# Attention and a two-layer MLP on one core: six instead of eight column groups of the first layer beside attention

## The chip, the core and the metric

The kernel runs on one core of a Trainium2 chip. TensorE (PE) multiplies, VectorE (DVE), ScalarE (ACT) and GpSimd (POOL) do the element-wise work, and SyncE (SP) issues nearly all DMAs. The metric is the time of one execution in microseconds (us); the median of several runs counts.

## What is computed

```python
scores = scale * q @ k.T            # 4 batches, 8 heads, 576 tokens, head size 64
scores = where(block_i >= block_j, scores, -1e9)      # causal in blocks of 64 tokens
attn = exp(scores - max) / (sum + 1e-9)
x = (attn @ v), heads side by side  # 2304 tokens x 512
h = x @ w_in;  x = (max(h, 0) + alpha * min(h, 0)) @ w_out     # 512 -> 2048 -> 512
h = x @ w2_in; out = (h * sigmoid(1.702 * h)) @ w2_out         # 512 -> 2048 -> 512
```

The weights arrive as 64-bit floats and are narrowed on the chip. Every product of the two layers is made from split numbers: a high part that the PE takes exactly and a low part, so that three products (high by high, high by low, low by high) stand for one.

## The kernel before

**Attention** runs in 20 passes of two heads. The first eight (batch 0, in two halves) turn their exponentials with the PE: `score` writes PSUM tile `sc`, `soft` takes the minimum (DVE) and the exponential (ACT), `turn_e` transposes the exponentials into PSUM, `turn_out` copies them out (ACT), `pv_t` multiplies by `v`. The other twelve passes turn them by a DMA transpose (`pt<-hl`, three a pass, 36 in all) and `pv` reads them. At the start the PE has little to do and 104 dummy products (`warm`) are put in.

**The first layer** has 16 column groups of 128. The first `NA` of them, eight, are computed beside attention, for eight blocks of 288 tokens, whenever the attention has finished a block: `gemm1` (tile `h`, 12 matmuls a group) and `g2_half` (tile `x`). These matmuls of 288 columns are what fills the PE between the steps of attention; the text calls them the fill. Their partial result goes to DRAM (`xa`). The other eight groups come after attention, two groups (a pair) at a time, for units of 512 tokens (four whole ones and a half): `first_half` and `second_half` form seven products of 256 columns in place of eight (tiles `ga`, `ep`), `snap` and `sums` put them together, and `g2` multiplies on into four PSUM banks `acc`. At a unit's end `block_out` loads the partial result (`o<-xa`), adds it to the four banks on DVE and stores the sum (`x2s<-o`). There are two `o` buffers for the four banks, so the loads for the third and fourth bank wait until the first two stores have landed.

**The second layer** works like the second part of the first, with all 16 groups as eight pairs.

The combined weights of the seven products are made by `comb`, stored to DRAM (`wc<-wc`) and loaded again (`ws<-wc`, 256 KB each). Before, the four pairs of the first layer are loaded once and stay in place; those of the second layer are loaded again for each unit.

`narrow` turns a 64-bit weight tile into 32 bits: one ACT operation and three on DVE. `gate` computes the activation: for the second layer a sigmoid on ACT and a product on DVE.

**The order** on each engine is fixed when the kernel is built. `at` notes every step with a due time plus a number from the table `SHIFT`; `arrange` is a list scheduler that goes through a model of the five engines and always takes the ready step with the smallest number. SP's DMAs too stand in one such order, and a DMA that waits for its data holds up those behind it.

Of the kernel before, what the change touches and what calls it, by code (L numbers as in the profile page):

```python
# [52 lines left out]

ORDER = {
# [6 lines left out]
    "comb 2": 232.8, "comb 3": -27.9, "first": 27.3, "gate": -98.0, "gate 0": -19.6, "gate 2": 67.8,  # L61
    "gemm1": 68.3, "gemm1 0": 171.6, "gemm2": 27.6, "half": 66.8, "half 0": 164.8, "half out": -68.7,
    "half out 0": 90.2, "high": 37.1, "load alpha": -25.6, "load k": 97.5, "load k 0": -174.1, "load q": 31.3,
    "load q 0": 127.5, "load v": -31.6, "load v 0": 140.7, "load w": -98.2, "load w 2": -24.0,
    "load w 3": 13.9, "load wc": -36.6, "load x": 132.4, "narrow": 100.5, "narrow 2": 19.6, "narrow 3": 96.5,
    "norm": 32.7, "norm 0": 111.8, "out": 26.7, "out t": -34.5, "prep out": 33.8, "prep out 0": 43.8,
    "prep t": 63.8, "prep t 0": -50.0, "prep v": 92.2, "pv": -64.1, "pv out": -63.9, "pv t": 43.2,
    "rest": -30.8, "scale t": 6.7, "score": -10.7, "score 0": -166.4, "second": 27.7, "setup": -15.8,
    "setup 2": -29.8, "snap": 1.4, "soft": -70.8, "soft 0": 17.8, "split g": -167.4, "split g 0": 68.9,
    "split g 2": 45.0, "split w": -71.7, "split w 2": 46.4, "split w 3": 58.0, "split x": 35.9,  # L70
    "split x 2": 84.1, "sum out": -41.5, "sum t": 28.5, "sums": -46.2, "turn": -70.2, "turn out": -30.2,
    "warm": 50.2,
# [5 lines left out]
def kernel(  # L78
# [19 lines left out]
    NA = 8  # L98
# [133 lines left out]
    def gate(key, layer, f):  # L232
        ps, n = pend[key, f]
        g = gbuf(key, "g")[:, 0:n]
        to = ps if key[0] else g
        if layer == 0:
            act.activation(out=g, in_=ps, func=ACTF.Relu, scale=-1.0)
            dve.scalar_tensor_tensor(out=to, in0=g, scalar=nalph[:, f:f + 1], in1=ps, op0=ALU.mult, op1=ALU.add)  # L238
        else:
            act.activation(out=g, in_=ps, func=ACTF.Sigmoid, scale=1.702)  # L240
            dve.tensor_tensor(out=to, in0=g, in1=ps, op=ALU.mult)
        pend[key, f] = (to, n)
# [10 lines left out]
    def plan_g1(n, key, layer, f, lo):  # L253
        z = " 0" if key[1] < 2 else ""
# [24 lines left out]
    def plan_block(i, where):  # L279
# [4 lines left out]
        for z, (d, e) in enumerate(G2):  # L284
            x = " 0" if i < 2 else ""
# [207 lines left out]
    def turn_out(i, g, t):  # L493
        ps, n = st.pop(("et", i, g, t)), len(TURN[g][t])
        if n == 8:
            st[i, "pt", g, t] = two.tile([128, 9, 128], F32, tag="pt", bufs=PTB, name="pe")
            hi_part(st[i, "pt", g, t][:, 0:8], ps)
# [112 lines left out]
    for u, (i, g, prods, part) in enumerate(slots):  # L610
        n = place_[u]
        lag = 5 if i >= N0 else 4
        x = " 0" if i < NTP else ""
# [638 lines left out]
```

## Time and profile before

| | us |
|---|---|
| median of 3 runs | 1004.37 (1003.66 to 1005.82) |
| the profiled execution | 1003.02 |
| its span, first to last instruction | 1001.2 |
| PE busy | 978.1 (98%) |
| DVE, ACT, POOL busy | 651.0, 533.7, 351.9 |

The span falls into five stretches. To 117.4 us the first eight passes run; to 350.5 us the passes with DMA transposes; to 413.9 us only what is left of the fill; to 621 us the pairs of the first layer; and then the second layer. "Busy" of the PE overlaps from one matmul to the next, so the pace of a run of matmuls is read from their starts.

### The profile page before, as it was taken

What the parts mean: (1) busy time and instruction counts of PE and PEld (TensorE: products, weight loads), DVE (VectorE), ACT (ScalarE), POOL (GpSimd) and SP (SyncE); (2) the same over time, 40 slices, a digit from 0 to 9 for tenths busy, and PEclk for the clock granted to TensorE, in tenths of its full rate; (3) what the DMA queues carried; (4) which work ended last, traced back from release to release, by engine and by line L of the source; (5) the groups of instructions that cost most, each with busy time, mean ns of one, the idle gap of its engine ahead of it and who ended that gap; (6) DMA issues with size and microseconds to landing.
All of it is one profiled execution on the core that took longest, in us unless ns stands there. A gap on an engine that the chain in (4) does not pass through costs nothing.

```text
span 1001.2 us, 21866 instructions
## 1 busy us (share of the span) xinstructions
PE 978.1 (98%) x8260; PEld 859.7 (86%) x8260; DVE 651.0 (65%) x1301; ACT 533.7 (53%) x1284; POOL 351.9 (35%) x396
## 2 busy tenths in 40 slices
PE   8999999999999999999999999999999999999998
PEld 5777787787788999999899889889999899899997
DVE  4788877786577566778778797887535534534332
ACT  4778777775777455565445555555423423433232
POOL 4346243442625156753426535233311311211000
PEclk9999999999999999999999999999999999999999
DMA  9635999999986866654656688987745756564360
GB/s 191 161 124 142 209 211 205 206 204 213 192 201 131 169 210 218 243 190 167 206 171 230 231 274 273 315 302 248 238 160 181 256 165 198 195 207 145 98 208 32
DMA packets 234648, 198.31 MB, mean 198 GB/s; under 512 B 146224, under 2 KB 172848, under 8 KB 234544
## 3 DMA queue, kind: packets, MB, share of 16 engines
q1 hardware_dynamic: 233216, 196.60, 69.2%
q8 instruction: 65, 1.06, 0.5%
q10 hardware_dynamic: 1328, 0.33, 0.2%
q14 instruction: 39, 0.32, 0.1%
HBM read 136.32 MB, written 40.89 MB: 177 GB/s over the span
## 4 chain that ended last, share of the span: by engine, by line
PE 81%; DMA 9%; ACT 3%; DVE 2%; POOL 2%; SPq 1%; issue 1%; POOLq 0%; ACTq 0%; DVEq 0%
PE acc L918 28%; PE ga L843 15%; PE ep L843 11%; PE h L223 7%; PE pv L599 3%; PE sc L448 3%; DMA pt<-hl 3%; PE x L268 3%; PE x L269 3%; PE x L270 3%; DMA wc<-wc 3%; PE pv L524 2%; PE tp L388 1%; DMA o<-xa 1%; PE s L448 1%
## 5 line engine op out<-in xcount | busy, mean ns | idle before, releaser
L918 PE MATMUL acc<-wh,gs 128*128 128x512 f32 x576 | 184.5, 391 | 2.1 <-DVE o L928 2.1
L843 PE MATMUL ga<-xc,ws 128*128 128x256 f32 x1368 | 184.2, 283 | 0.0
L843 PEld LDWEIGHTS ga<-xc,ws 128*128 128x128 f32 x1368 | 176.5, 191 | 4.6
L843 PE MATMUL ep<-xc,ws 128*128 128x256 f32 x936 | 130.7, 283 | 0.0
L918 PEld LDWEIGHTS acc<-wh,gs 128*128 128x128 f32 x576 | 108.3, 188 | 24.6 <-DVE o L928 2.9
L869 POOL TENSOR_TENSOR v<-u,v 128x256 f32<-128x256 f32 x48 | 40.5, 843 | 239.4 <-ACT v L868 239.3
L843 PEld LDWEIGHTS ep<-xc,ws 128*128 128x128 f32 x936 | 120.4, 192 | 0.4
L918 PE MATMUL acc<-wl,gs 128*128 128x512 f32 x288 | 112.6, 391 | 0.0
L867 ACT ACTIVATE u<-ga 128x512 f32<-128x512 f32 x48 | 28.6, 596 | 146.3 <-PE ga L843 146.3
L918 PE MATMUL acc<-gs,wh 128*128 128x512 f32 (+1 forms) x320 | 92.2, 371 | 2.1 <-DVE o L928 2.1
L891 DVE TENSOR_TENSOR u<-ep,v 128x256 f32<-128x256 f32 x48 | 20.2, 421 | 112.0 <-PE ep L843 111.7
L143 POOL TENSOR_TENSOR gs<-g,gs 128x288 fp32r<-128x288 f32 x64 | 56.1, 881 | 100.8 <-ACT gs L140 95.8
L223 PE MATMUL h<-xh,wh 128*128 128x288 f32 x256 | 78.8, 308 | 1.2 <-DVE g L238 1.1
L268 PE MATMUL x<-gs,wh 128*128 128x288 f32 x256 | 76.9, 304 | 0.5 <-ACT xo L274 0.3
L223 PE MATMUL h<-xlb,wh 128*128 128x288 f32 x256 | 77.1, 301 | 0.0
L269 PE MATMUL x<-gs,wh 128*128 128x288 f32 x256 | 76.2, 299 | 0.5 <-POOL gs L143 0.5
L223 PE MATMUL h<-xh,wl 128*128 128x288 f32 x256 | 76.4, 298 | 0.0
L270 PE MATMUL x<-gs,wl 128*128 128x288 f32 x256 | 76.1, 300 | 0.0
L462 DVE TENSOR_REDUCE stat<-sc 128x1 f32<-128x384 f32 (+7 forms) x128 | 55.1, 457 | 24.0 <-PE sc L448 22.2
L472 ACT ACTIVATE e<-sc,stat 128x384 f32<-128x384 f32 (+7 forms) x128 | 64.1, 511 | 7.4 <-DVE stat L462 6.6
L822 POOL TENSOR_TENSOR xt<-xr 128x512 f32<-128x512 f32 x40 | 55.2, 1389 | 35.6 <-DVE xc L143 13.5
L918 PEld LDWEIGHTS acc<-gs,wh 128*128 128x128 f32 x320 | 56.8, 189 | 11.2 <-DVE o L928 2.7
(118 smaller groups left out, 2146.6 us busy)
## 6 DMA issues: line engine op xcount, KB each, us to landing
ws<-wc SPq DMA_DIRECT2D x284, 256.0 KB, 3.9
wc<-wc SPq DMA_DIRECT2D x84, 256.0 KB, 3.3
rw<-in_moe_w_in_dram SPq DMA_DIRECT2D x32, 512.0 KB, 4.4
rw<-in_moe_w_out_dram SPq DMA_DIRECT2D x32, 512.0 KB, 4.1
xa<-xo SPq DMA_DIRECT2D x32, 144.0 KB, 3.3
out_dram<-o SPq DMA_DIRECT2D x18, 256.0 KB, 2.4
nat_k<-in_k_dram SPq DMA_DIRECT2D x32, 128.0 KB, 3.0
vt<-in_v_dram SPq DMA_DIRECT2D x32, 128.0 KB, 3.3
```

Source lines behind the costliest of these rows:

```text
L143: eng.tensor_tensor(out=dst, in0=src, in1=hi.bitcast(F32), op=ALU.subtract)
L223: pe.matmul(ps, st_[:, sl], mv[:, c], start=z == 0, stop=z == 3 * KD - 1)
L268: pe.matmul(ps, oh[:, sl], gh, start=f == 0, stop=False)
L269: pe.matmul(ps, oh[:, sl], gl, start=False, stop=False)
L270: pe.matmul(ps, ol[:, sl], gh, start=False, stop=f == NA - 1)
L448: pe.matmul(to[x:x + 64], qs[64 * h:64 * h + 64, 64 * y:64 * y + 64], ks[64 * h:64 * h + 64, k0:k0 + n], start=True, stop=True)
L462: dve.tensor_reduce(out=stat[:, 0, a:a + 1], in_=v, op=ALU.min, axis=AX.X if y < 8 else AX.XY)
L472: act.activation(out=eo if y < 8 else eo.rearrange("p (a b) -> p a b", a=2), in_=v, func=ACTF.Exp, scale=-1.0, bias=stat[:, 0, a:a + 1], a ...
L822: pool.tensor_tensor(out=x, in0=y, in1=y2, op=op)
L843: pe.matmul(ps, st_, mv, start=first and z == 0, stop=last and z == 5, skip_group_check=True)
L869: pool.tensor_tensor(out=v, in0=u[:, TH:TB], in1=v, op=ALU.subtract)
L918: pe.matmul(ps, a, b_, start=first and z == 0, stop=last and z == 2)
```

## The change

- `NA` goes from 8 to 6. Beside attention there are six groups; after it five pairs of the first layer, so ten pairs' halves by seven products, where there were eight.
- All pairs of the first layer are loaded from DRAM for every unit, as in the second layer, into three slots used in turn (`slot`, `load_wc`).
- The first four passes put their turned exponentials into two banks of the layers' pool (one is the dummy products' bank) and no longer into a buffer of the scores.
- `narrow` has two DVE operations in place of three, `gate` of the second layer one ACT operation and none on DVE.
- `SHIFT` has own numbers for the batches of attention and for the two layers; all its numbers are new, so the whole order changes.

```diff
-    NA = 8
+    NA = 6
@@ narrow
-        act.activation(out=sq, in_=wf[:, :, 1], func=ACTF.Copy, scale=2.0 ** -112)
+        act.activation(out=sq, in_=wf[:, :, 1], func=ACTF.Prelu, scale=2.0 ** -112, alpha=2.0 ** 32)
...
-        dve.tensor_scalar(out=a, in0=hi, scalar1=3, scalar2=0x7FFFFFF8, op0=ALU.logical_shift_left,
-                          op1=ALU.bitwise_and)
-        dve.scalar_tensor_tensor(out=a, in0=hi, scalar=-0x80000000, in1=a, op0=ALU.bitwise_and, op1=ALU.bitwise_or)
-        dve.scalar_tensor_tensor(out=hi, in0=wi[:, :, 0], scalar=29, in1=a, op0=ALU.logical_shift_right,
-                                 op1=ALU.bitwise_or)
+        dve.tensor_scalar(out=a, in0=wi[:, :, 0], scalar1=29, scalar2=7, op0=ALU.logical_shift_right, op1=ALU.bitwise_and)
+        dve.scalar_tensor_tensor(out=hi, in0=hi, scalar=3, in1=a, op0=ALU.logical_shift_left, op1=ALU.bitwise_or)
@@ gate
-            act.activation(out=g, in_=ps, func=ACTF.Sigmoid, scale=1.702)
-            dve.tensor_tensor(out=to, in0=g, in1=ps, op=ALU.mult)
+            act.activation(out=g, in_=ps, func=ACTF.Gelu_apprx_sigmoid)
@@ turn_e
+        if g == 0 and t == 0:
+            ps = [st.pop("warm"), bank("et")]
+            for u, (c, y) in enumerate(us):
+                pe.transpose(ps[u // 4][:, u % 4 * 128:u % 4 * 128 + 128], st[i, "e", y][:, 128 * c:128 * c + 128], ident)
+            st["et", i, g, t] = ps
+            return
@@ slot
-        if z < 3:
-            pl, tag = (wts_a, f"{'hl'[z - 1]}0_{i}") if z else (late["w"], f"s{i}")
-        else:
-            pl, tag = wts_a, f"{'hl'[i % 2]}1_{NA // 2 + i // 2}"
+        f, y = divmod(7 * z + i, 2)
+        pl, tag = (wts_a, f"{'hl'[y]}0_{f}") if f < NA else (late["w"], f"s{z}_{i}")
@@ load_wc
-        if l == 0 and j in wc0:
-            wc[p] = wc0[j]
-            return
-                t = slot(j if l == 0 else (p - P2) % NSL, i)
+                t = slot(p % NSL, i)
-        if l == 0:
-            wc0[j] = ts
@@ SHIFT
-    "gemm1": 68.3, "gemm1 0": 171.6, "gemm2": 27.6, "half": 66.8, "half 0": 164.8, "half out": -68.7,
+    "gemm1 b2": 73.3, "gemm1 b3": 73.3, "gemm2": 27.2, "gemm2 1": 29.7, "half": 74.7, "half 0": 57.4,
```

Over the whole program the PE's order has 768 `h` and 768 `x` matmuls before and 576 and 576 now; 2304 of `ga` and `ep` before and 2496 now; 1248 `acc` matmuls of 512 columns before and 1344 now, and 96 of 256 columns before and 120 now. SP has 284 `ws` loads before and 416 now. The 36 transposes and the 104 dummy products stay. Of the fill, 196 matmuls before and 124 now stand ahead of the first `pv` that reads a DMA transpose, 836 and 754 between this one and the last `pv`, and 504 and 274 behind it. ACT's order has two ACT_TABLE_LOADs before and two now.

PE, first two passes, before (`k_266` holds the keys, `qt_184` and `qt_185` are the queries of the first and the second pass; the dummy products between are left out):

```order
L448 MATMUL sc<-k_266,qt_184 64x64 x2
L388 MATMUL tp<-ident,nat_k_177 128x128 x3
L388 MATMUL tp<-ident,nat_q_175 128x128 x3
...
L490 MATMUL et<-ident,e 128x128 x3
L448 MATMUL sc<-k_266,qt_185 64x320 x2
```

The same place now (`qt_191`, `qt_192` are the queries):

```order
L460 MATMUL sc<-k_273,qt_191 64x64 x2
L400 MATMUL tp<-ident,nat_k_184 128x128 x3
L400 MATMUL tp<-ident,nat_q_182 128x128 x3
...
L460 MATMUL sc<-k_273,qt_192 64x320 x2
...
L501 MATMUL et<-ident,e 128x128 x3
```

The second pass's scores moved ahead of the first pass's transposes.

SP, among the first loads, before (`vt` takes the values, `rw` a 64-bit weight tile):

```order
L158 DMA rw<-in_moe_w_in_dram 128x4x128
L677 DMA nalph<-in_moe_alpha_dram 128x16x1
L359 DMA nat_q_175<-in_q_dram 64x4x64
L359 DMA nat_q_176<-in_q_dram 128x4x64 x2
L359 DMA nat_q_176<-in_q_dram 64x4x64
L359 DMA nat_k_177<-in_k_dram 128x4x64 x2
L158 DMA rw<-in_moe_w_in_dram 128x4x128
L359 DMA nat_k_177<-in_k_dram 128x4x64
L359 DMA vt_179<-in_v_dram 128x4x64 x3
```

The same place now:

```order
L172 DMA rw<-in_moe_w_in_dram 128x4x128
L371 DMA nat_q_182<-in_q_dram 64x4x64
L371 DMA vt_186<-in_v_dram 128x4x64 x3
L371 DMA nat_q_183<-in_q_dram 128x4x64 x2
L371 DMA nat_q_183<-in_q_dram 64x4x64
L172 DMA rw<-in_moe_w_in_dram 128x4x128
L371 DMA vt_187<-in_v_dram 128x4x64 x3
```

The first three loads of values moved ahead of the second weight tile and of the other query loads.

SP, at the end of the first unit of the first layer, before:

```order
L929 DMA x2s<-o 128x512 x2
L158 DMA rw<-in_moe_w_in_dram 128x4x128
L927 DMA o<-xa 128x512
L753 DMA wc_3_0_127<-wc 128x512
L158 DMA rw<-in_moe_w_in_dram 128x4x128
L753 DMA wc_3_1_128<-wc 128x512
L927 DMA o<-xa 128x512
```

The same place now:

```order
L939 DMA x2s<-o 128x512 x2
L799 DMA ws<-wc_4_6_112 128x512
L799 DMA ws<-wc_4_4_110 128x512
L799 DMA ws<-wc_4_3_109 128x512
L172 DMA rw<-in_moe_w_in_dram 128x4x128
L937 DMA o<-xa 128x512
L772 DMA wc_2_0_127<-wc 128x512
L799 DMA ws<-wc_1_0_85 128x512
L799 DMA ws<-wc_0_2_80 128x512
L799 DMA ws<-wc_1_1_86 128x512
L772 DMA wc_2_1_128<-wc 128x512
L799 DMA ws<-wc_0_5_83 128x512
```

Loads of combined weights came in between the stores and the two loads that follow them; the second `o<-xa` stands right behind the last row shown.

## Rows read from the trace of the kernel before

**Rows 1.** The page: busy time by engine, and the chain that ended last, by engine.
```profile
PE 978.1 (98%) x8260; PEld 859.7 (86%) x8260; DVE 651.0 (65%) x1301; ACT 533.7 (53%) x1284; POOL 351.9 (35%) x396
PE 81%; DMA 9%; ACT 3%; DVE 2%; POOL 2%; SPq 1%; issue 1%; POOLq 0%; ACTq 0%; DVEq 0%
```

**Rows 2.** Busy us (count) by stretch: PE, PEld, DVE, ACT, POOL; clock, DMA, GB/s.
```profile
0.00:117.40 117.40, 112.21 (x1088) 84.02 (x1088) 89.62 (x201) 81.72 (x213) 50.19 (x77) 0.99 0.65 161
350.50:413.90 63.40, 62.84 (x476) 62.18 (x470) 40.07 (x57) 36.01 (x85) 41.55 (x40) 1.00 0.68 226
413.90:621.00 207.10, 205.04 (x1353) 188.86 (x1353) 166.85 (x300) 108.14 (x228) 98.55 (x104) 1.00 0.65 219
```

**Rows 3.** What the PE waited for: total us, times, longest.
```profile
PE pv L599 <- DMA pt<-hl: 5.9, 6, 1.8
PE pv L524 <- DMA vt<-in_v_dram: 2.0, 1, 2.0
PE acc L918 <- DVE o L928: 4.1, 4, 1.7
```

**Rows 4.** PE in order of time: start, us, line, operation; pieces of three runs.
```profile
62.09 0.30 PE L223 MATMUL h<-xh,wh 128*128 128x288 f32 x1
64.75 0.29 PE L223 MATMUL h<-xh,wl 128*128 128x288 f32 x1
...
720.67 1.60 PE L843 MATMUL ga<-xc,ws 128*128 128x256 f32 x12
722.11 1.60 PE L843 MATMUL ep<-xc,ws 128*128 128x256 f32 x12
723.55 0.40 PE L918 MATMUL acc<-wh,gs 128*128 128x512 f32 x1
...
729.02 1.59 PE L843 MATMUL ga<-xc,ws 128*128 128x256 f32 x12
```

**Rows 5.** The stretches of the passes with DMA transposes, columns as in rows 2.
```profile
117.40:298.00 180.60, 171.54 (x2340) 139.46 (x2339) 129.15 (x309) 128.79 (x373) 70.89 (x75) 1.00 1.00 207
298.00:350.50 52.50, 52.32 (x685) 46.86 (x681) 32.92 (x76) 33.40 (x99) 19.04 (x22) 1.00 0.70 149
```

**Rows 6.** `narrow` and the second layer's gate: count, busy us, mean ns, idle before.
```profile
L177 DVE SCALAR_TENSOR_TENSOR sq<-rw,wa 128x512 int32<-128x512 int32 x64 | 53.0, 828 | 1.2
L241 DVE TENSOR_TENSOR ga<-g,ga 128x512 f32<-128x512 f32 (+1 forms) x40 | 25.7, 642 | 30.2 <-ACT g L240 30.1
```

**Rows 7.** DMA issues, median us to landing: whole page; transposes, 117.4 to 298 us.
```profile
ws<-wc SPq DMA_DIRECT2D x284, 256.0 KB, 3.9
...
pt<-hl SPq DMA_TRANSPOSE x28, 5.5
```

**Rows 8.** Loaded and unloaded stretches of the layers, columns as in rows 2.
```profile
505.00:520.00 15.00, 15.00 (x112) 14.34 (x111) 9.31 (x22) 6.12 (x17) 3.94 (x6) 1.00 0.60 210
575.00:595.00 20.00, 17.94 (x118) 16.21 (x117) 17.57 (x33) 9.98 (x19) 6.92 (x7) 1.00 0.88 298
610.00:620.00 10.00, 10.00 (x66) 9.12 (x65) 6.17 (x11) 6.15 (x11) 6.89 (x7) 1.00 1.03 373
628.00:645.00 17.00, 14.92 (x84) 12.52 (x83) 14.64 (x25) 8.04 (x16) 4.48 (x5) 1.00 1.01 348
```

**Rows 9.** DVE's additions into `o` at two unit ends, in order of time.
```profile
506.59 0.69 DVE L928 TENSOR_TENSOR o<-acc,o 128x512 f32<-128x512 f32 x1
514.93 0.68 DVE L928 TENSOR_TENSOR o<-acc,o 128x512 f32<-128x512 f32 x1
...
576.03 1.28 DVE L928 TENSOR_TENSOR o<-acc,o 128x512 f32<-128x512 f32 x2
586.65 0.69 DVE L928 TENSOR_TENSOR o<-acc,o 128x512 f32<-128x512 f32 x1 [0.55 <-DMA o<-xa]
```

**Rows 10.** PE in order of time at two unit ends, with the idle time before.
```profile
587.40 0.73 PE L918 MATMUL acc<-gs,wh 128*128 128x512 f32 x2 [1.60 <-DVE o L928]
636.45 0.50 PE L918 MATMUL acc<-wh,gs 128*128 128x512 f32 x1 [1.71 <-DVE o L928]
```

More of the change, by code (lines that the diff above doesn't have):

```diff
@@ L51 @@
 ]
+STAGE = (" 0", "", " b2", " b3", " b4")
 ORDER = {
@@ L253, in plan_g1 @@
     def plan_g1(n, key, layer, f, lo):
-        z = " 0" if key[1] < 2 else ""
+        z = STAGE[key[1] // 2]
         at("gemm1", n, lambda: gemm1(key, layer, f), z)
@@ L496, in turn_out @@
             st[i, "pt", g, t] = two.tile([128, 9, 128], F32, tag="pt", bufs=PTB, name="pe")
-            hi_part(st[i, "pt", g, t][:, 0:8], ps)
+            if g == 0:
+                for x in range(2):
+                    hi_part(st[i, "pt", g, t][:, 4 * x:4 * x + 4], ps[x].rearrange("p (u k) -> p u k", k=128))
+            else:
+                hi_part(st[i, "pt", g, t][:, 0:8], ps)
         else:
@@ L612 @@
         lag = 5 if i >= N0 else 4
-        x = " 0" if i < NTP else ""
+        x = STAGE[4 if NP <= i < N0 else passes[i][0]]
         at("score", n, lambda u=u: score(u), x)
@@ L649 @@
                     used[i, nm] = n
-            x = " 0" if i < NTP else ""
+            x = STAGE[4 if NP <= i < N0 else passes[i][0]]
             at("prep t", n, lambda i=i, z=z: prep_t(i, z), x)
@@ L653 @@
         for piece in range(2 if i >= NTP else 0):
-            at("prep v", f0 - 1 + piece, lambda i=i, piece=piece: prep_v(i, piece))
+            at("prep v", f0 - 1 + piece, lambda i=i, piece=piece: prep_v(i, piece), STAGE[passes[i][0]])
     def at_load(n, nm, *a, queue=sp):
-        at("load " + nm, n, lambda: load(nm, *a, queue), " 0" if a[1] == 0 else "")
+        at("load " + nm, n, lambda: load(nm, *a, queue), STAGE[a[1]])
     for x in range(2):
@@ L738, in comb @@
                 6: (a12, a22, ALU.subtract)}
-        kept = l == 0 and j >= PRE
-        t = slot(j, i) if kept else raw.tile([128, 2, 256], F32R, tag="wc", bufs=2, name="wc")
+        t = raw.tile([128, 2, 256], F32R, tag="wc", bufs=2, name="wc")
         lo = pool if i % 2 else dve
@@ L826, in comb_x @@
         if i == 2 and odd:
-            t = [wts_a.tile([128, 2, TH], F32R, tag=f"{y}0_{NA - 1}", name="xc") for y in "hl"]
+            t = [late["w"].tile([128, 2, TH], F32R, tag=f"xc{y}", name="xc") for y in "hl"]
         else:
@@ L946 @@
         n, key = place[p], u[3]
-        at("load wc", place[max(p - 2, 0)] - 4 * (p < 2), lambda p=p: load_wc(p))
-        at("first", n, lambda p=p: first_half(p))
-        at("snap", n + 0.3, lambda p=p: snap(p))
-        at("second", n + 0.9, lambda p=p: second_half(p))
-        at("sums", n + 1.3, lambda p=p: sums(p))
+        at("load wc", place[max(p - 2, 0)] - 4 * (p < 2), lambda p=p: load_wc(p), "" if l == 0 else " 1")
+        at("first", n, lambda p=p: first_half(p), "" if l == 0 else " 1")
+        at("snap", n + 0.3, lambda p=p: snap(p), "" if l == 0 else " 1")
+        at("second", n + 0.9, lambda p=p: second_half(p), "" if l == 0 else " 1")
+        at("sums", n + 1.3, lambda p=p: sums(p), "" if l == 0 else " 1")
         for y, f in enumerate(fpair(l, j)):
             z = 2 * (p % 2) + y
-            at("gate 2", n + 1.4, lambda key=key, l=l, f=f: gate(key, l, f))
-            at("split g 2", n + 1.4, lambda key=key, f=f, z=z: gate_split(key, f, dve, z))
-            at("gemm2", place[p + 2] + 0.1 + 0.1 * y, lambda u=u, f=f, a=j == 0 and y == 0, b=j == NPAIR[l] - 1 and y == 1: g2(u, f, a, b))
+            at("gate 2", n + 1.4, lambda key=key, l=l, f=f: gate(key, l, f), "" if l == 0 else " 1")
+            at("split g 2", n + 1.4, lambda key=key, f=f, z=z: gate_split(key, f, dve, z), "" if l == 0 else " 1")
+            at("gemm2", place[p + 2] + 0.1 + 0.1 * y, lambda u=u, f=f, a=j == 0 and y == 0, b=j == NPAIR[l] - 1 and y == 1: g2(u, f, a, b), "" if l == 0 else " 1")
         if j == NPAIR[l] - 1:
-            at("out", place[p + 2] + 0.4, lambda u=u: block_out(u))
+            at("out", place[p + 2] + 0.4, lambda u=u: block_out(u), "" if l == 0 else " 1")
     for u in units:
@@ L969 @@
     seq_w += [(t_end + NR + 1 + (n3 + QL - t_end - NR) * j / NPAIR[1], 1, j, None) for j in range(NPAIR[1])]
-    seq_w += [(n3 - QC + 2 * f if f < NA // 2 else n3 + f - NA // 2, 1, None, f) for f in range(NF)]
+    seq_w += [(n3 - QC + 2 * f if f < NA else n3 + f - NA, 1, None, f) for f in range(NF)]
     at_w = 0
```

63 lines of the change are left out of this document (29 added, 34 removed), and 11 rows, old and new, of the table SHIFT.

## The prediction

> **What bounds the kernel now.** I read the page first: the PE is busy for 978.1 of 1001.2 us, no other engine for more than 65%, and 81% of the chain that ended last is PE [rows 1]. So time is won where PE work goes, or where a wait of the PE goes, and nowhere else. The table by stretch says where the PE has slack [rows 2, 5]: it is at 99% behind attention (62.84 of 63.40 us) and in the first layer (205.04 of 207.10), and looser before, 5.2 us idle in the first 117.4 us and 9.1 us in the 180.6 us that follow. The list of the PE's own waits names the causes [rows 3]: DMA transposes that land late (5.9 us), the load of values at the start (2.0 us), and in the layers the four banks of a unit's end (4.1 us). One more view matters, the DMA share: 1.00 in the 180.6 us of the passes with DMA transposes, 0.70 in their last 52.5 us [rows 5], 0.65 in the first layer [rows 2].
>
> **The change part by part.**
>
> *PE work removed.* Two groups less beside attention take away 192 `h` and 192 `x` matmuls of 288 columns. From 62.09 to 64.75 us one such run has 20 steps in 2.66 us, so one takes 0.133 us [rows 4]. 384 x 0.133 = 51.1 us.
>
> *PE work added.* A fifth pair costs, by the counts of the order, 192 more matmuls of 256 columns in seven products, 96 more `acc` of 512 and 24 more of 256. Twelve of 256 columns take 1.44 us (720.67 to 722.11), 0.120 each; 24 of 512 take 5.47 us (723.55 to 729.02), 0.228 each [rows 4]. 216 x 0.120 + 96 x 0.228 = 25.9 + 21.9 = 47.8 us. Net: **-3.3 us**. This is certain as long as the PE stays as dense as it is.
>
> *Where the removed fill stood.* The order tells: 72 of the 384 ahead of the first `pv` of a DMA transpose, 82 between this and the last `pv`, 230 behind it: 9.6, 10.9 and 30.6 us. The 30.6 us go for sure, since the PE does nothing else there [rows 2]. The 9.6 us at the start go if the other engines can follow: DVE is at 89.6 and ACT at 81.7 of 117.4 us there [rows 2], and both lose work, so I take them as gone; the other end is that nothing of them is gained, +9.6. Of the 10.9 us, 41 matmuls, 5.5 us, lie in the stretch with DMA share 1.00 [rows 5]. The transposes stay 36, and between the first and the last of them SP's order has 3 `wc` and 4 `xa` stores more and 2 weight tiles less, so the DMA engines would have to do the same work in 3% less time. I take this as done, because DMA shares of 1.01 and 1.03 stand in other stretches [rows 8]; the other end is +5.5.
>
> *First passes' banks, and the order at the start.* The second pass's scores no longer wait for the first pass's transposes. The PE loses nothing by two copies more. What I count is the load of values: its first part now stands ahead of a 512 KB weight tile and of six query and key loads on SP, so the PE's wait for it should go: **-2.0 us** [rows 3]. The bounds are 0 (the loads moved behind it are late in its place) and -2.0.
>
> *DVE and ACT.* `narrow` loses one DVE operation: the two kinds left and the one removed are between about 0.5 and 0.83 us, the costliest being 828 ns [rows 6], so 64 of them take away 30 to 53 us of DVE. The second layer loses 80 products of 642 ns [rows 6], 51 us. No engine but the PE bounds those places, so I take 0 for both; the PE's 5.9 us of waits for transposes [rows 3] are the most that faster DVE work could give back, since a transpose waits for DVE's low parts. The order shows as many table loads on ACT as before, so the two new functions cost nothing there. Fewer `gate` and split operations beside attention go the same way.
>
> *132 more loads of combined weights.* The first layer's stretch moves 219 GB/s in 207.1 us, 45.4 MB [rows 2]. 132 loads of 256 KB [rows 7] add 34.6 MB. In 207.1 + 47.8 = 254.9 us, 80 MB ask for 314 GB/s. The best ten microseconds that the trace shows are at 373, the loaded 17 us at 348 [rows 8], so the loads themselves fit, with little room. What the load does to others is seen at a unit's end. With a DMA share of 0.60 the third bank's addition comes 8.3 us after the first (506.59, 514.93) and the PE waits for nothing; with 0.88 it comes 10.6 us after (576.03, 586.65) [rows 8, 9], and the PE waits 1.60 us there, and 1.71 us at the next end, share 1.01 [rows 8, 10]. The first layer has five such ends, of which two are loaded now (4.1 us in all, [rows 3]). From the old unit's last `acc` to the first `acc` of the third bank the order has products for 7.9, 7.3, 6.5, 9.0 and 13.3 us before and 9.1, 7.0, 10.0, 8.4 and 12.1 us now: 2.6 us more in all. More load and a little more room: I take the 4.1 us as they are. The bounds: none of the five waits (-4.1), or each needs the 10.6 us that the first loaded end needed (9.0 + 1.6) and the last 15.0 (13.3 + 1.7): waits of 1.5, 3.6, 0.6, 2.2 and 2.9, 10.8 in all, and 0.4 each for the fourth bank ((4.1 - 3.3) / 2), 12.8, so +8.7.
>
> A rule of the Trainium skill speaks against these loads: "DMA: Bandwidth & Descriptors", in its section "Bandwidth", asks for transfers of 1 MiB or more to reach three quarters of the peak and puts 64 KB at 138 GB/s. By it 256 KB lies below the 314 GB/s asked for or barely at it; the trace's 373 GB/s speaks for the other reading.
>
> *The sum.* -3.3 - 2.0 = -5.3 us on a span of 1001.2. The profiled execution took 1003.02 us, 1.8 more than its span, and the median is 1004.37; I take the difference off the median: **999.0 us**.
>
> **The rivals.**
>
> 1. *Attention does not contract.* With less fill the PE comes to the `pv` sooner and stands there until the transpose lands. For it: the DMA share of 1.00 and the 5.9 us of such waits [rows 3, 5]. Against it: DVE, whose low parts the transposes need, gets lighter. It decides once the transposes follow one another no faster than now, some 6.4 us apart (28 in 180.6 us, [rows 7]). If only that stretch stays: 999.0 + 5.5 = 1004.5, no change. If the start stays too: 1014.1.
> 2. *Unit ends under load, slower.* SP's order has new `ws` loads between the stores and the loads of `o`; with the stretch at 314 GB/s all five ends are loaded. Price +8.7 as worked out: 1007.7 us. It decides where an `o` load lands later than the 7.0 to 12.1 us of products reach. For it: both loaded ends waited [rows 10]. Against: three ends without a wait.
> 3. *Both waits go.* DVE's relief brings the transposes in time (-5.9) and the unit ends fit (-4.1): 989 us. For it: the lighter DVE. Against: nothing takes load off the DMA engines.
> 4. *The loads don't queue well.* If the first layer's stretch moved no more than its 219 GB/s of now, 80 MB would take 365 us in place of 255: 1109 us. Against: 298 to 373 GB/s in three stretches [rows 8]. The rule of the skill named above is this rival's.
> 5. *The start gains nothing.* Only the -3.3 us stay: 1001.1, inside the forecast's own range.
>
> **How the numbers follow.** The forecast with rival 5, 996 to 1002.3: 0.44. Rival 3, 988 to 996: 0.14. Rival 1 in its weak form, 1002.4 to 1006.3: 0.15. Rival 2, rival 1 in its strong form and parts of both, 1006.4 to 1015: 0.25. Rival 4: 0.02. A measurement of this kernel tells about 0.2%, 2 us, from no change. So faster 0.58, same 0.15, slower 0.27. The range for eight in ten runs from 988.5, rival 3's price, to 1010, which leaves out the strong ends of rivals 1 and 2 and rival 4.
>
> **What would show it.** Right: the PE's first `pv` of a DMA transpose near 106 us in place of 117.4, the last near 330, the first `ga` near 363, and the first layer then some 255 us long with a DMA share near 0.9; no wait for `vt` at the start. Wrong: the PE's wait for `pt` grown by 5 us or more and the twelve passes as long as now (rival 1); waits of `acc` for `o` above 6 us (rival 2), or waits of `ga` and `ep` for `ws`, which are in no row now (rival 4).

## The result

The changed kernel is slower: 1018.4 us median of four runs (1015.17 to 1020.75), against 1005.1 for the kernel before, run beside it (1003.66 to 1006.13). The ratio is 1.0131, with a 95% interval of 1.0097 to 1.0166. The forecast was 999.0, its range ended at 1010. The profiled execution took 1020.75 us, on a span of 1018.9.

The table by stretch, cut at the same four events as before (first and last `pv` of a DMA transpose, first `ga`, last `acc` of the first layer), has these rows in the changed kernel; columns as in rows 2, and it is to be read beside rows 2 and 5.

```profile
0.00:107.00 107.00, 101.50 (x1009) 73.88 (x1009) 66.22 (x173) 73.94 (x195) 45.87 (x75) 0.98 0.76 176
107.00:333.80 226.80, 215.27 (x2946) 176.14 (x2946) 166.62 (x380) 163.96 (x481) 94.49 (x96) 1.00 0.96 204
333.80:371.30 37.50, 35.49 (x269) 34.52 (x261) 23.42 (x37) 24.47 (x56) 26.47 (x25) 1.00 0.89 314
371.30:637.60 266.30, 255.12 (x1641) 232.38 (x1642) 183.94 (x327) 125.32 (x264) 112.31 (x118) 0.99 0.92 311
637.60:1018.90 381.30, 374.87 (x2336) 338.51 (x2335) 143.16 (x270) 152.76 (x296) 73.93 (x81) 1.00 0.60 197
```

Its first number behind the times is the length of a stretch, the second the PE's busy time. Set against the forecast, stretch by stretch:

| stretch | before, us | after, us | difference | forecast |
|---|---|---|---|---|
| start, to the first `pv` of a transpose | 117.4 | 107.0 | -10.4 | -11.6 |
| passes with transposes | 233.1 | 226.8 | -6.3 | -10.9 |
| fill behind them | 63.4 | 37.5 | -25.9 | -27.5 |
| first layer | 207.1 | 266.3 | +59.2 | +44.7 |
| the rest | 380.2 | 381.3 | +1.1 | 0 |
| span | 1001.2 | 1018.9 | +17.7 | -5.3 |

The forecast's 30.6 us behind the last `pv` are split here, since 207 of those 230 matmuls stand ahead of the first `ga` (27.5 us) and 23 behind it (3.1 us, so 47.8 - 3.1 = 44.7 in the first layer). Two rows carry the miss: **14.5 us in the first layer and 4.6 in the passes with transposes**.

The page's busy time by engine answers to the first line of rows 1, and its DMA issues of combined weights to that of rows 7:

```profile
PE 982.3 (96%) x8188; PEld 855.4 (84%) x8188; DVE 583.3 (57%) x1183; ACT 540.5 (53%) x1290; POOL 353.1 (35%) x393
...
ws<-wc SPq DMA_DIRECT2D x416, 256.0 KB, 4.3
```

The PE is busy for 4.2 us more, where the forecast's sum had 3.3 us less work for it. What the difference is made of is read from the stretches below. The PE's waits (total us, times, longest), beside rows 3:

```profile
PE acc L928 <- DVE o L938: 10.4, 8, 4.2
PE pv L622 <- DMA pt<-hl: 8.8, 9, 1.8
...
PE ga L853 <- ACT u L877: 1.9, 3, 1.3
```

The wait for `vt` is gone, as forecast. The wait of the unit ends has gone from 4.1 to 10.4 us, that for transposes from 5.9 to 8.8.

**One unit end, step by step.** First the answers for the tile `o` over the first layer and its end: in the kernel before, then in the changed one. The lines say what DVE waited for at its additions (us, times), and the time from issue to landing, over `o`'s stores and loads together.

```profile
  DMA o<-xa: 1.2, 2
...
DMA to landing us min/median/max: 1.7/3.1/7.0
```

```profile
  DMA o<-xa: 14.6, 7
...
DMA to landing us min/median/max: 2.0/4.9/6.7
```

Then the first unit end of the changed kernel: SP's queue, DVE's additions and the PE, each in order of time (start, length, engine, line, operation, idle time before); at the end the landing times of the two stores and of the load.

```profile
434.51 0.92 SPq L939 DMA_DIRECT2D x2s<-o  x2
435.58 2.14 SPq L799 DMA_DIRECT2D ws<-wc  x3
437.82 0.52 SPq L172 DMA_DIRECT2D rw<-in_moe_w_in_dram  x1
441.23 0.32 SPq L937 DMA_DIRECT2D o<-xa  x1
...
433.80 1.28 DVE L938 TENSOR_TENSOR o<-acc,o 128x512 f32<-128x512 f32 x2
447.38 0.69 DVE L938 TENSOR_TENSOR o<-acc,o 128x512 f32<-128x512 f32 x1 [4.83 <-DMA o<-xa]
...
448.12 1.15 PE L928 MATMUL acc<-gs,wh 128*128 128x512 f32 x2 [4.18 <-DVE o L938]
...
DMA to landing us min/median/max: 6.7/6.7/6.7
...
DMA to landing us min/median/max: 6.1/6.1/6.1
```

Two banks are added at 433.80 and stored from 434.51. Each store lands 6.7 us after its issue; only then is its buffer of `o` free, and the load for the third bank goes out at 441.23. That lands 6.1 us later, DVE adds at 447.38, and the PE, which wants the bank for the next unit, has stood for 4.18 us. The third addition comes 13.6 us after the first. At the loaded end of before it came after 10.6 us, at an unloaded one after 8.3 [rows 9].

**What follows such a wait.** Stretches around the first two unit ends, PE alone: length, PE busy, granted clock, DMA share, GB/s; then the longest wait of the second end.

```profile
440.00:447.40 7.40, 3.94 (x28) 1.00 0.93 303
448.10:455.00 6.90, 6.88 (x27) 0.75 0.82 274
499.00:506.00 7.00, 4.60 (x36) 1.00 0.97 342
506.00:512.00 6.00, 6.00 (x39) 0.72 1.05 385
...
505.79 0.50 PE L928 MATMUL acc<-gs,wh 128*128 128x256 f32 x2 [1.78 <-DVE o L938]
```

The PE is busy for 3.94 of 7.40 us, then fully busy at a granted clock of 0.75: about half of the 6.90 us lie at the lower of the two levels, 1.2 GHz. At the second end the PE stands for 0.62 and then 1.78 us, and a clock of 0.72 follows. The Trainium skill describes such a fall in "TensorE: Matmul & The Clock Gate", section "HAM oscillation — how this bites in real kernels": a PE that idles for a DMA between bursts starts the next burst cold. The trace agrees at these two ends, with 4.18 us of idle time ahead and 0.75 behind at the first. It is not so behind every wait: from 512 us to the layer's end, with waits for `o` of 0.40 to 1.15 us, the clock is 1.00, and the kernel before shows 1.00 around its waits of 1.60 and 1.71 us [rows 8, 10].

So the 14.5 us in the first layer are two things. Its idle time rose from 207.10 - 205.04 = 2.1 us to 266.30 - 255.12 = 11.2, which is 9.1 more; 9.7 of the 11.2 are waits of `acc` for `o`. And the PE's busy time is 255.12 where 205.04 and 44.7 of work make 249.7: 5.4 us more. The lower clock accounts for some 3.4 of them, an estimate from the two rows (6.90 x 0.25 + 6.00 x 0.28).

### The profile page after: what moved, and what is told of

Same layout as the page of the kernel before. It is cut to its first block, busy times and chain, and to the rows that moved or that the text cites. A ratio compares the mean times of both kernels' runs of the same rounds, so it can differ in the third digit from the quotient of the medians.

```text
span 1018.9 us, 21986 instructions
## 1 busy us (share of the span) xinstructions
PE 982.3 (96%) x8188; PEld 855.4 (84%) x8188; DVE 583.3 (57%) x1183; ACT 540.5 (53%) x1290; POOL 353.1 (35%) x393
## 4 chain that ended last, share of the span: by engine, by line
PE 45%; DMA 4%; DVE 1%; ACT 1%; SPq 1%; issue 1%; POOL 0%; DVEq 0%; ACTq 0%; POOLq 0%
PE acc L928 24%; PE ga L853 12%; PE ep L853 8%; DMA o<-xa 3%; DMA xr<-x2s 1%; SPq L799 0%; DVE o L938 0%; DMA x2s<-o 0%; DVE wc L157 0%; POOL xt L832 0%; ACT L253 0%; DVE xc L157 0%; DVE u L901 0%; ACT gs L154 0%; DVE wc L767 0%
## 5 line engine op out<-in xcount | busy, mean ns | idle before, releaser
L157 DVE TENSOR_TENSOR gs<-g,gs 128x512 fp32r<-128x512 f32 (+1 forms) x80 | 55.2, 690 | 163.5 <-ACT gs L154 163.4
L928 PE MATMUL acc<-gs,wh 128*128 128x512 f32 (+1 forms) x400 | 117.8, 378 | 9.7 <-DVE o L938 9.7
L154 ACT ACTIVATE gs<-g 128x512 fp32r<-128x512 f32 (+2 forms) x128 | 68.3, 534 | 107.5 <-PE acc L928 101.8
L928 PE MATMUL acc<-gs,wl 128*128 128x512 f32 (+1 forms) x200 | 74.8, 374 | 0.0
L832 POOL TENSOR_TENSOR xt<-xr 128x512 f32<-128x512 f32 x40 | 56.3, 1414 | 30.9 <-DMA xr<-xs 13.2
L474 DVE TENSOR_REDUCE stat<-sc 128x1 f32<-128x320 f32 (+7 forms) x128 | 54.6, 456 | 17.9 <-PE sc L460 16.2
L596 DVE SCALAR_TENSOR_TENSOR hl<-e,stat,hl 128x448 f16<-128x448 f32 (+8 forms) x108 | 60.0, 603 | 8.3 <-ACT hl L591 7.3
L928 PEld LDWEIGHTS acc<-wl,gs 128*128 128x128 f32 x288 | 54.2, 188 | 9.8
L767 POOL TENSOR_TENSOR wc<-sq 128x256 f32<-128x256 f32 x39 | 32.9, 845 | 84.2 <-DMA wc<-wc 42.6
L235 PE MATMUL h<-xh,wh 128*128 128x288 f32 x192 | 59.3, 309 | 2.8 <-DVE g L250 2.5
L622 PEld LDWEIGHTS <-vp 128*64 128x64 bf16 x1680 | 46.1, 111 | 16.9 <-issue 9.3
```

The lines of the kernel that those rows point to most:

```text
L154: act.activation(out=dst, in_=src, func=ACTF.Copy, scale=scale_)
L157: eng.tensor_tensor(out=dst, in0=src, in1=hi.bitcast(F32), op=ALU.subtract)
L235: pe.matmul(ps, st_[:, sl], mv[:, c], start=z == 0, stop=z == 3 * KD - 1)
L474: dve.tensor_reduce(out=stat[:, 0, a:a + 1], in_=v, op=ALU.min, axis=AX.X if y < 8 else AX.XY)
L596: dve.scalar_tensor_tensor(out=hl_part(part, y, 1), in0=e, scalar=stat[:, 2, a:a + 1], in1=hl_part(part, y, 0), op0=ALU.mult, op1=ALU.subt ...
L622: pe.matmul(o, l, r, start=z < 2, stop=z >= len(ops) - 2)
```

## The experiments

Theory L says that the bytes of the 132 added loads make `o`'s stores and loads late, and that the rest follows. Its first rivals: the new order itself (O), or added work dearer than I worked out (W). The kernel's planner lays out every engine's order anew for each edit. Where a label begins with p_, it was replaced by lists, so each engine does its work in exactly the order of the changed kernel (p_bnarrow: of the kernel before). The others are planned anew. Ratios are to the kernel before on the same chip.

### The bytes alone

```diff
+        if l == 0 and p >= NPAIR[0]:
+            wc[p] = base[p % NSL]
+            for i in range(7):
+                if n == TB or i in (2, 3, 5, 6):
+                    sp.dma_start(out=wc[p][i].bitcast(F32).rearrange("p h c -> p (h c)")[0:1], in_=wcs[l][j][i][0:1])
+            return
```

> The changed kernel, in which the first layer's 125 loads of combined weights behind the first unit carry one partition (2 KB) in place of 128 (256 KB); the tiles keep the first unit's weights, so the values of the other four units are left out. The order of all engines stays as good as the same. Theory L (in the first layer the DMA engines are so busy that the load of o, which waits for the store of the o two banks earlier, comes late; the PE stands at each unit's end and runs at its lower clock for a while behind it): the waits of acc for o fall from 10.4 to under 3 us, no stretch of the layer has a granted clock under 0.99, first ga to last acc of the layer takes 250 to 254 us in place of 266.4, total 1003 to 1007. Rival O (the new order itself is at fault, the additions stand too late in DVE's row): waits and time as in the changed kernel, 1015 to 1020. Rival W (the added products cost more than I worked out): the layer as long as now with the PE busy, 1015 to 1020.

> The changed kernel with every engine's order held, in which the first layer's 125 weight loads behind the first unit carry one partition (2 KB) in place of 128; the tiles keep the first unit's weights, so the other units' values are left out. Only the bytes differ. If the bytes alone make the first layer's excess (theory L): first ga to last acc 251 to 254 us in place of 266.4, waits of acc for o under 3 us, total 1003 to 1008. If the order has a share in it: 255 to 262 us, total 1009 to 1014.

a_noload: 1009.65 us, ratio 1.0043 (1.0017 to 1.0070); the layer 252.7 us. p_noload: 1007.51 us, ratio 1.0013 (0.9994 to 1.0032), as expected of the bytes alone. The first layer's stretch in p_noload, columns as above, and the PE's wait:

```profile
373.90:625.70 251.80, 250.47 (x1641) 229.75 (x1642) 182.09 (x327) 125.91 (x267) 109.91 (x118) 1.00 0.60 201
...
PE acc L936 <- DVE o L946: 2.0, 3, 0.9
```

With the same order and the same matmuls, the layer takes 251.8 us: 207.1 + 44.7. The waits fall to 2.0 us, the granted clock is 1.00, and PE busy time is back from 255.12 to 250.47. O and W fall here: the bytes make all of the 14.5 us, and against this run they are 9.9 us of idle time (11.2 for 1.3) and 4.65 of busy time, 3.4 of it the lower clock as estimated above; the other 1.2 I don't explain. That the layer meets the forecast's work to a tenth is partly luck: the PE is busy 0.7 us longer than the 249.7 worked out, and idle 0.7 us less than in the kernel before. a_noload's total is above its expected 1003 to 1007; in its profiled execution the layer is 13.6 us shorter than the changed kernel's, but the other stretches together 2.6 us longer, which I don't explain either.

### The series of store and load

```diff
-            o = late["x"].tile([128, DM], F32, tag="o", bufs=2, name="o")
+            o = (late["x"] if d < 2 else tmp_p).tile([128, DM], F32, tag="og"[d // 2 % 2], bufs=2, name="o")
```

> The changed kernel with four buffers for o in place of two, so that no load of o waits for a store; the DMA load stays whole. Theory L: the loads of all four banks have landed before the unit ends, the waits of acc for o fall from 10.4 to under 3 us, the clock stays up, total 1004 to 1009 (10 to 14 us less than the changed kernel). Should the DMA share alone delay other loads too, 1010 to 1013. Rival O (DVE's row): the additions stand where they stood, waits above 7 us, 1014 to 1019. Rival W: 1015 to 1020.

> The changed kernel with every engine's order held and four buffers for o: the loads of the third and fourth bank no longer wait for a store, but stand where they stood on SP. By theory L the series of store and load costs one transfer per unit end: the waits of acc for o fall from 10.4 to 2 to 5 us, the layer to 257 to 261 us, total 1010 to 1014. If the loads come too late even so, since they are issued behind the stores: waits above 8 us, total 1015 to 1019.

a_o4: 1013.76 us, ratio 1.0077 (1.0057 to 1.0096). Its PE has no wait for `o` at all, but others in their place; then the layer, a stretch of it, and the landing of the six `ws` loads between 473 and 485 us:

```profile
PE ga L853 <- ACT u L877: 4.0, 6, 1.7
...
PE ga L853 <- ACT u L883: 1.8, 1, 1.8
PE ep L853 <- ACT v L878: 1.7, 1, 1.7
...
373.60:632.90 259.30, 253.51 (x1641) 230.60 (x1642) 185.36 (x327) 125.67 (x265) 110.20 (x118) 0.99 0.93 322
470.00:500.00 30.00, 26.52 (x158) 23.32 (x158) 24.99 (x44) 15.78 (x36) 14.16 (x13) 0.94 0.88 298
...
DMA to landing us min/median/max: 5.1/7.9/9.1
```

The layer takes 259.3 us, 7.0 less than the changed kernel and 7.5 more than without the bytes. The wait of 1.8 us is put down to ACT, whose copy starts at 483.18 and takes 0.39 us, so it ended by 483.57; a `ws` load issued at 474.6 with 9 us to land is due at the same moment. Which of the two ended last the profile can't decide. In any case the weights' loads themselves now land 5 to 9 us after issue, and the clock falls to 0.94 in this stretch. This is the expectation's 1010 to 1013 for the case that the share delays other loads too, and a little more.

p_o4: 1017.0 us, ratio 1.0123 (1.0087 to 1.0159), a total that can't be told from the changed kernel's, as expected for loads that come too late even so. The waits of `acc` for `o` are still 8.8 us, though the layer is 6.0 us shorter. Its waits and its layer, then SP's queue, which shows why the waits stay:

```profile
PE acc L928 <- DVE o L938: 8.8, 7, 2.4
...
373.10:633.40 260.30, 253.47 (x1642) 230.99 (x1643) 180.23 (x328) 126.24 (x268) 112.24 (x118) 0.99 0.94 320
...
437.63 0.92 SPq L939 DMA_DIRECT2D x2s<-o  x2
438.64 2.08 SPq L799 DMA_DIRECT2D ws<-wc  x3
440.83 0.41 SPq L172 DMA_DIRECT2D rw<-in_moe_w_in_dram  x1
441.29 0.50 SPq L937 DMA_DIRECT2D o<-xa  x1
```

The third bank's load needs no store now, and still goes out at 441.29, behind stores, weights and a raw tile, 3.7 us behind the store where it was 6.7. So with the order held the waits get shorter (2.4 us at most, for 4.2) and don't go; they go in a_o4, where the planner moved the loads forward. In the layer the two differ by 1.0 us only, since a_o4 has waits of `ga` in their place. Why the totals differ by 3.2 us isn't shown; p_o4's four runs spread from 1015.17 to 1023.62.

### Fewer bytes, with the values kept

```diff
-    jobs = [(u[0], u, j) for u in units for j in range(NPAIR[u[0]])]
+    jobs = [(u[0], u, j) for y, u in enumerate(units) for j in range(NPAIR[u[0]])[::-1 if u[0] == 0 and y % 2 else 1]]
...
-            if n == TB or i in (2, 3, 5, 6):
-                t = slot(p % NSL, i)
...
+        for i in sorted(todo_l[p]):
+            ts[i] = slot(spot[p], i)
```

`todo_l[p]` lists the tiles of the pair that lie in no slot yet, `spot[p]` is the slot chosen for it.

> The changed kernel with every second unit of the first layer going through the five pairs backwards, so that the two or three pairs that lie in the three slots at a unit's end serve the next unit without a load: 69 of the 160 loads go, 18 MB, and around a unit's end there are none. Theory L: stores and loads of o land in 2 to 3.5 us there, the waits of acc for o fall to 2 to 5 us, total 1005 to 1010. Rival O: 1013 to 1020 with waits above 7 us. Rival W: 1015 to 1020.

> Both edits in one: the pairs backwards in every second unit (69 loads less) and four buffers for o. With four buffers alone the first layer took 259.4 us from first ga to last acc, with 125 loads less 252.7. Theory L, in its present form: the two causes are the series of store and load through two buffers and, once that is gone, loads of ws and xr that land 7 to 9 us after issue; here neither is left, so no wait of acc for o, none of ga for ws over 1 us, granted clock 1.00 throughout, the layer 252 to 255 us, total 1006 to 1010. Rival Q (the loads that stay, those of the second layer's weights and combinations among them, fill the queue anyway): waits of 4 us and more on ga and ep, the layer 257 to 260, total 1011 to 1015.

a_serp: 1018.51 us, ratio 1.0114 (1.0082 to 1.0146): a miss. Its layer, and its wait:

```profile
371.00:634.30 263.30, 255.07 (x1641) 232.58 (x1642) 192.48 (x342) 132.46 (x280) 113.84 (x120) 0.99 0.76 258
...
PE acc L940 <- DVE o L950: 10.9, 7, 3.5
```

Taking 18 MB off brought the share from 0.92 to 0.76, and the waits stayed at 10.9 us: `o`'s transfers still took 4.0 us to land by the median, up to 7.8, where I had expected 2 to 3.5. The second layer's raw weights and combinations still move there; and a bank still takes two landings in series, whatever the load is by the mean. a_serp_o4, with both edits, took 1007.45 us, ratio 1.0003 (0.9986 to 1.0020), with no wait for `o` and none for `ws`:

```profile
371.10:623.50 252.40, 251.25 (x1641) 229.92 (x1642) 184.83 (x335) 130.40 (x275) 114.67 (x119) 1.00 0.78 267
```

The layer is at 252.4 us, at full clock, with nothing left out. Either edit alone gave 3 and 7 us, both together 13.9, nearly all that is to be had. Rival Q falls.

### The bytes in the kernel before

```diff
-        if l == 0 and j in wc0:
+        if l == 0 and j == 0 and j in wc0:
             wc[p] = wc0[j]
```

> The kernel before, in which three of the four pairs of the first layer are loaded again for each unit into the same tiles instead of being kept: 75 loads, 19.7 MB more, and nothing else. With the 45.4 MB of its first layer that asks for 314 GB/s, as the changed kernel does. Theory L: waits of acc for o grow from 4.1 to 9 to 14 us, the total from 1005 to 1010 to 1017. Rivals O and W: the load alone costs nothing that can be seen, 1004 to 1007.

b_stream3: 1035.33 us, ratio 1.0338 (1.0269 to 1.0406), far over the expectation. Its first layer and the rest, and its two largest waits:

```profile
412.80:634.60 221.80, 211.28 (x1355) 192.59 (x1354) 160.88 (x285) 104.88 (x220) 97.73 (x100) 0.98 0.82 279
634.60:1028.60 394.00, 381.18 (x2336) 341.60 (x2334) 202.42 (x377) 150.31 (x299) 76.70 (x84) 0.99 0.60 196
...
PE acc L918 <- DVE o L928: 9.6, 7, 3.1
PE acc L918 <- ACT wh L140: 8.2, 3, 6.5
```

In the layer 75 loads cost 221.8 - 207.1 = 14.7 us, with waits for `o` of 9.6 us in all and a clock of 0.98. That is as much as the changed kernel's excess, without the change; but this kernel is planned anew, so it supports theory L and doesn't show it by itself. The other half came later: in the new plan the second layer's `wh` was late (8.2 us, and up to 18 us longer in the rest). This I had not expected.

### The passes with transposes

```diff
+        if l == 0 and j:
+            sp.dma_start(out=wcs[l][j][i][0:1], in_=t.bitcast(F32).rearrange("p h c -> p (h c)")[0:1])
...
-                sp.dma_start(out=t.bitcast(F32).rearrange("p h c -> p (h c)"), in_=wcs[l][j][i])
+                sp.dma_start(out=t.bitcast(F32).rearrange("p h c -> p (h c)"), in_=wcs[l][j if l else 0][i])
```

> The changed kernel, in which the stores of the first layer's combined weights of pairs 1 to 4 carry one partition in place of 128, 7.3 MB less in the passes with DMA transposes, and the loads of the first layer read pair 0's weights in place of the others'; what is left out is the other pairs' values. Theory M (the passes with transposes contract by less than their fill because the DMA engines at a share of 0.98 to 1.00 set the pace of the transposes): first to last pv of a transpose 226.8 us to 220 to 223, waits for pt from 8.8 to under 5 us, total 1012 to 1015. Rival H (what paces them is the work of ACT and DVE on the high and low parts): the stretch within 1.5 us of 226.8, waits for pt 8 us or more, total 1016 to 1020.

> The thin stores once more (pairs 1 to 4 store one partition, all units read pair 0's weights, the other pairs' values are left out), now with every engine's order held as in the changed kernel, since without that 21 fill matmuls had moved into the stretch. Theory M (the DMA engines set the pace of the passes with transposes): first to last pv of a transpose from 226.8 to 220 to 224 us, waits for pt from 8.8 to under 6 us, the whole 1012 to 1016. Rival H (ACT's and DVE's work on the parts, or the queue's own order, sets it): the stretch 225.5 to 228, waits for pt 8 us or more, total 1015 to 1020.

a_thinwc, planned anew: 1025.86 us, ratio 1.0189 (1.0167 to 1.0211), as neither theory said: the planner had moved 21 fill matmuls into the stretch, which came out at 230.7 us. It settles nothing. p_thinwc, in the changed kernel's order: 1013.11 us, ratio 1.0059 (1.0038 to 1.0081). The stretch and the wait:

```profile
106.60:326.30 219.70, 214.10 (x2942) 175.84 (x2944) 168.05 (x381) 163.83 (x481) 92.95 (x96) 1.00 0.89 177
362.90:622.30 259.40, 251.72 (x1642) 229.82 (x1642) 180.25 (x327) 125.21 (x265) 111.63 (x118) 1.00 0.94 320
...
PE acc L931 <- DVE o L941: 8.1, 5, 3.4
PE pv L622 <- DMA pt<-hl: 4.5, 5, 1.9
```

With 7.3 MB off, the stretch is 7.1 us shorter and the waits are halved. PE busy time fell by 1.2 us only, so it is mostly idle time that went. This profile is of the fastest of ten runs, and its total is 8 us under their median; but the stretch measures 226.6 to 228.7 us in the three kernels with this order and DVE work that keep those stores, whatever their totals, so 219.7 lies well outside. The medians say the same: ratio 1.0059 for the changed kernel's 1.0131, some 7 us. Theory M holds: the DMA engines set the pace there, and the stores of combined weights are a part of it.

This execution is fast in the first layer too, the second row: 259.4 us for 266.3, with the changed kernel's order and as many bytes. Half of that is PE busy time, 251.72 us for 255.12, as much as the lower clock was put at above: the PE waits for `o` here too, 3.4 us at the longest, but the granted clock is 1.00 over the layer. So the lower clock follows such a wait in some executions and not in others, and its price is no fixed one.

### DVE's relief

For a_oldng the new lines of `narrow` and of the second layer's gate give way to the old ones; for b_parts the old ones, and `turn_e` and `turn_out`, to the new:

```diff
-        act.activation(out=sq, in_=wf[:, :, 1], func=ACTF.Prelu, scale=2.0 ** -112, alpha=2.0 ** 32)
+        act.activation(out=sq, in_=wf[:, :, 1], func=ACTF.Copy, scale=2.0 ** -112)
...
-            act.activation(out=g, in_=ps, func=ACTF.Gelu_apprx_sigmoid)
+            act.activation(out=g, in_=ps, func=ACTF.Sigmoid, scale=1.702)
+            dve.tensor_tensor(out=to, in0=g, in1=ps, op=ALU.mult)
```

> The kernel before with the other parts of the change and without the six groups: the narrowing with two operations on DVE, the one-instruction gate of the second layer, and the first passes' exponentials transposed into the layers' banks. My prediction put these at 0 to -5.9 us for DVE's relief and -2.0 for the values' wait, which went by the order of loads and not by the banks. If the forecast's reading holds (only PE bounds): 1003 to 1006, no difference that can be told; if DVE's relief brings the transposes in time: 999 to 1002 with the waits for pt under 3 us; if the planner's order comes out worse by the edit: 1007 and more.

> The changed kernel with the narrowing and the gate of before (three DVE operations and a product on DVE more). I put 0 for this relief. If that is right: 1016 to 1021, as the changed kernel. If the relief is what lets the loaded layer and the passes go on at all: 1022 to 1030, with the PE's waits for pt at 12 us or more or new waits of acc for wh.

b_parts (the kernel before with these parts of the change, in its own plan): 1023.48 us, ratio 1.0179 (1.0154 to 1.0203). a_oldng (the changed kernel with the old narrowing and gate): 1079.98, ratio 1.0723 (1.0699 to 1.0746), with 13.2 us of waits for `wh`. Both are planned anew. In b_parts 67 fill matmuls more stand in the passes with transposes (903 for 836), which take 247.7 us; a kernel with less work on DVE and 17 us slower tells of its plan, not of the parts. I take both as inconclusive, and held the order for the next two.

```diff
         dve.tensor_scalar(out=a, in0=wi[:, :, 0], scalar1=29, scalar2=7, op0=ALU.logical_shift_right, op1=ALU.bitwise_and)
+        dve.tensor_scalar(out=a, in0=wi[:, :, 0], scalar1=29, scalar2=7, op0=ALU.logical_shift_right, op1=ALU.bitwise_and)
+        dve.tensor_scalar(out=a, in0=wi[:, :, 0], scalar1=29, scalar2=7, op0=ALU.logical_shift_right, op1=ALU.bitwise_and)
```

This is p_dve; p_bnarrow puts the new lines of `narrow` alone into the kernel before.

> The changed kernel, every engine's order held, with the first of narrow's two DVE operations done three times (128 operations of some 0.43 us, 55 us of DVE work more, about what the change took off); values as before. My forecast put DVE's relief at 0 in the time. If so: 1016 to 1021. If DVE's relief was worth time that hid in the sum, it comes back here: 1023 to 1035, with waits for pt above 12 us or new waits of acc for wh.

> The kernel before with the new narrowing alone (64 DVE operations and some 64 us of DVE work less), every engine's order held as in the kernel before. My forecast put this relief at 0, with 5.9 us of waits for pt as the most that it can give. If it is worth nothing where only the PE bounds: 1004.5 to 1007. If DVE bounds places of the start and the passes that no PE wait shows: 996 to 1002.

p_bnarrow: 1008.34 us, ratio 1.0014 (0.9993 to 1.0036), a little over its expected 1004.5 to 1007: in the order of before the narrowing's relief is worth nothing that can be measured. p_dve: 1042.82 us, ratio 1.0363 (1.0344 to 1.0382), 24 us over the changed kernel and above even the upper expectation. Its profiled execution is the fastest of four, 18.4 us over the changed kernel's; its first three stretches:

```profile
0.00:112.30 112.30, 102.96 (x1010) 73.61 (x1012) 81.49 (x201) 74.59 (x195) 46.88 (x75) 1.00 0.70 168
112.30:342.40 230.10, 216.97 (x2946) 177.09 (x2946) 174.34 (x398) 163.67 (x481) 93.14 (x96) 0.99 0.96 200
342.40:386.90 44.50, 38.44 (x271) 36.34 (x265) 38.70 (x54) 24.72 (x57) 27.02 (x25) 0.96 0.76 269
```

Put back, the work costs 5.3 us at the start, 3.3 in the passes and 7.0 behind them. So the relief pays nothing by itself, but the smaller fill needs it: in this order the gains of 10.4 and 25.9 us would have been some 5 and 19 without it.

### A version against both kernels

```diff
-    PTB = 2
+    PTB = 3
```

> Pairs backwards in every second unit and four buffers for o, and besides three buffers for a transpose's result in place of two, so that a transpose can be issued one pass earlier. Theory B (a transpose waits for its buffer): waits for pt from 9.1 to under 4 us, first to last pv 221 to 224 us, total 1001 to 1004. Rival D (the DMA engines or the parts set the pace): the stretch within 1.5 us of 227, total 1005 to 1009.

> As the one with three buffers for the transpose's result, and four in place of three for the exponentials e, so that the scores of a pass may run further ahead. Theory B2 (e's buffers hold back ACT and so the parts): waits for pt under 3 us, the stretch 219 to 223 us, total 999 to 1003. Rival D: no more than with three buffers, 1005 to 1009; should the planner put scores so early that the high and low parts come later, 1009 to 1014.

On top of a_serp_o4, three buffers for a transpose's result: 1004.76 us, ratio 0.9986 (0.9974 to 0.9999). With four for `e` as well: 1005.62, ratio 0.9983 (0.9970 to 0.9997). Their passes with transposes take 226.2 and 231.0 us, with waits for `pt` of 8.4 and 10.6 us. So theories B and B2 fall, and D stands, which fits p_thinwc. a_pt3 is 14 us under the changed kernel and at most a quarter of a per cent under the kernel before. The edits to the layer earned 11 of the 14, as a_serp_o4 has them alone; the other 2.7 lie within the spread of its runs (1003.08 to 1010.55), and a gain by the third buffer isn't shown.

## Why the prediction was wrong

*The PE's work* was right but for 0.7 us: 250.47 busy in the first layer without the bytes, 249.7 worked out. The wait for `vt` went, as put.

*The unit ends* are where it failed. I set the added 34.6 MB against the best rate in any stretch, found that they fit, and took the 4.1 us of waits as they were. They did fit: 311 GB/s against the 314 worked out, and rival 4 fell. With it falls, for these loads, what I had read out of the rule of the Trainium skill ("DMA: Bandwidth & Descriptors", section "Bandwidth") that stood beside it: the rule asks for transfers of 1 MiB, and here 311 GB/s were moved mostly in pieces of 256 KB. But fitting by rate is not landing in time: the median from issue to landing of `o` rose from 3.1 to 4.9 us, and a bank takes two landings in a row. **Rival 2 happened.** Its place was right, and of its two causes the load; the new `ws` entries between the stores and the loads cost nothing by themselves, as p_noload shows. Its price of +8.7 us is near the 9.1 of idle time in the layer, but partly by luck: it stood for waits of 12.8 us in all, with 4.0 at the second end and 1.9 at the first, and measured were 10.4 in all, with 2.4 and 4.2; the layer's idle time holds 1.9 us of waits of `ga` besides. It lacked a term: the lower clock behind two of the waits, some 3.4 us in this execution, and 1.2 of busy time that stay open. No row that I had read showed a fall of the clock behind a wait for `o`. And I gave it a part of 0.25, whose bounds ended at 1015, though both loaded ends of before had waited [rows 10] and the change loaded all five: "a little more room" in the order was weighed against landings that came out 1.8 us later by the median, twice in a row.

*The middle* was over-sized: 6.3 of 10.9 us. It is rival 1 in its weak form, priced at 5.5 and measured at 4.6. The share of 1.00 [rows 5] was in front of me, and I answered it with shares of 1.01 and 1.03 elsewhere [rows 8], which show that the engines can be full, not that there is room. p_thinwc shows the opposite.

*The start and the fill behind* came near: -10.4 for -11.6, -25.9 for -27.5. "For sure" was too strong, as p_dve shows: some 5 and 7 us of them rest on DVE's relief, which I had put at 0 as a gain. The 0 was right for the kernel before (p_bnarrow). It did not hold for the sum. Rivals 3 and 5 did not come: both waits grew, and the start gained.

Together: 999.0 + 14.5 + 4.6 = 1018.1, and 1018.4 was measured. That it comes so near is luck: the remaining 1.2, 1.6 and 1.1 us of the table are nearly cancelled by the 2.3 us by which this profiled execution lies above its median and the 1.4 by which that of before lay below its own; I don't explain them.

## What to carry to other kernels

Before adding transfers, don't ask only whether their bytes fit under the best rate that a trace shows: take the landing time of the loaded stretches, count how many landings stand in series ahead of the bounding engine, and give the waits a bound with the lower clock as well (here 3.4 us in one execution, none in another). A stretch with a DMA share near 1.00 need not shorten by all the work that the bounding engine loses: here it gave 6.3 of 10.9 us. And where a planner lays out the order, an edit is tested with the order held; planned anew, three of these runs told more of the plan than of the edit.

## What I had not expected of the hardware

- Clock: 4.18 us without work, then 0.75 of the full clock over the next 6.9 us; over the layer some 3.4 us, a third of what the idle time itself cost (9.9 against p_noload). But in p_thinwc a wait of 3.4 us was followed by the full clock, and here one of 1.78 us (0.62 shortly ahead of it) by 0.72: by the length of a wait alone the fall can't be told.
- Latency under load: at a share of 0.65 `o`'s transfers, most of them 256 KB, take 3.1 us to land by the median, at 0.92 4.9, at 0.78 (a_serp_o4) 4.2. "DMA: Bandwidth & Descriptors" of the Trainium skill, section "Latency and other measured facts", says that the fixed cost of a transfer grows with the load on HBM; the trace agrees in the direction, and its numbers may hold queueing too.
- Loads and stores side by side, some four fifths of their bytes in pieces of 256 KB, held 311 GB/s over 266 us, and 385 over 6.
